# Stores of the split rows moved to GpSimd's queue, the second block's rows fetched two units later, two splits made first

## The chip, the cores and the metric

The kernel runs on one core of a Trainium2 chip. The metric is the device time of one execution in microseconds; the median of three runs is given, and one further execution was profiled. The engines are named as in the profile: PE (TensorE's matmuls; PEld its weight loads), DVE (VectorE), ACT (ScalarE), POOL (GpSimd) and SP (SyncE, which here only issues DMAs; SPq is its queue). The 16 DMA engines of the core carry the transfers that a queue issues.

## The reference, cut to what matters

```python
attn_out = _attn_ref(q, k, v)            # 4 batches, 8 heads, 576 tokens, 64 channels a head; masked softmax attention
x = attn_out.transpose(0, 2, 1, 3).reshape(2304, 512)
h = np.maximum(np.maximum(x @ w1, x @ w2), x @ w3)   # 512 -> 768, three gates, their maximum
x = h @ w_out                                        # 768 -> 512
h = x @ w_in                                         # 512 -> 2048
g = np.maximum(h, 0.0) + alpha * np.minimum(h, 0.0)
out = g @ w_out2                                     # 2048 -> 512
```

All tensors are float32.

## The kernel before, in words

Every float32 matmul is made of three: an operand is split into a high part (a cast to the matmul's type `F32R`, on ACT) and a low part (operand minus high part, on DVE or GpSimd), and `PAIRS` (L728) multiplies high by high, high by low and low by high. `split` (L231) is that pair of instructions; in the profile its cast is L233 and its subtraction L236.

The program has three stretches. In the first, a planner (`Weave`) orders attention for all four batches and the first net (the three gates and `w_out`) for batches 0 to 2. The results of the first net are stored to DRAM (`x2d`, by `store_x2`). The second stretch is `last_net(3)` (L844), the first net for batch 3, written as a generator whose units are run one by one by the loop at L1126. The third is the second net, over three blocks of 768 tokens (L1469 on); its products are made by a scheme with seven half-size products in place of eight (`PRODUCTS`), which needs sums of quarter matrices.

`last_net` has 12 gate units (n = 0 to 11, L740), then six rounds k = 3 to 8 of seven products each (n = 12 to 53, L922), then eight output units (n = 54 to 61, L762). The rounds use the seven-product scheme too, so batch 3's tokens are summed first: `row_sums` (L863) writes quarter sums on DVE in units 1 to 4, and `make` splits them. There are eight such factors: T1, T2, T3 and T4, each for two column halves i. T1 lies in the tile of the row sums itself (a tile of the pools `xsp` for i = 0 and `xst` for i = 1), T2 to T4 in temporaries. The first product of a round is copied from its PSUM bank by ACT (L940); DVE adds the others to it (L902), and in rounds 5 and 8 the result goes through a cast (L935) and a subtraction (L909) to become `h`, which the output units read. There are eight PSUM banks, so PE can be eight products ahead of the engines that empty them.

Beside these units the loop prepares block 1 of the second net (tokens 768 to 1535), in two halves (0 and 1). `early_load` fetches a half's four row tiles from `x2d` (L991, SP's queue), `early_sums` makes its four sums on GpSimd (L1000, tiles `t` and `xs`), and `early_split` splits its seven factors, one every second unit, with the cast on ACT (L233, `xst<-xs` and `xst<-t`) and the subtraction on GpSimd (L236). `early_store`, called one unit after each split, stores the finished tile to DRAM (`xd`, L1029, SP's queue). The split tiles come from two pools of two buffers, taken in turn, so the fifth split of a half waits for the first's store to land. `X_SPLIT` sets the units: the load of half 0 stands at unit X_SPLIT - 8, its sums at X_SPLIT - 2 and its seven splits from unit X_SPLIT on; half 1 follows 21 or 22 units later. The two loaded tiles of a half lie in the two buffers of `xsp`, where the row sums for i = 0 lie before and the rows of block 0 come after (`load_x2` at L1139).

Block 2 is prepared in the same way in the second net (`high_part` on ACT, `low_part` on DVE), and `early_store` serves it as well, 14 stores for each block. Each engine runs its instructions in the order of the program, and so does SP's queue: an issue that waits holds up all issues behind it.

Of the kernel before, what the change touches and what calls it, by code (L numbers as in the profile page):

```python
# [10 lines left out]
F32 = mybir.dt.float32  # L11
F32R = mybir.dt.float32r
# [10 lines left out]
P = 128  # L23
# [5 lines left out]
HALF = S // 2  # L29
# [20 lines left out]
NOW = 9  # L50
NG = 3 * NF1 // 2
NP = 3
X_SPLIT = 10
COST = (250, 600, 500, 500)


# [116 lines left out]
def attention_maxout_prelu_kernel(  # L173
# [13 lines left out]
    nc = tc.nc  # L187
# [43 lines left out]
    def split(hi, lo, src, hi_engine, lo_engine):  # L231
        if hi_engine is nc.scalar:
            hi_engine.copy(hi, src)  # L233
        else:
            hi_engine.tensor_copy(hi, src)
        lo_engine.tensor_tensor(out=lo, in0=src, in1=hi.bitcast(F32), op=ALU.subtract)  # L236
# [5 lines left out]
    def pool(stack, name, bufs, side="left"):  # L242
        return stack.enter_context(tc.tile_pool(name=name, bufs=bufs, side=side, reuse_waits="tile"))
# [5 lines left out]
    xd = [None] + [[[dram.tile([P, 2, HB], F32, name=f"xd{blk}_{k}_{i}") for i in range(2)]  # L249
                    for k in range(7)] for blk in range(1, NBLK)]  # L250
# [7 lines left out]
    xp = pool(x0x, "xp", 10)  # L258
# [486 lines left out]
    def gate_unit(b, hf, f, g, st):  # L745
        acc = gate_products(b, hf, f, g)
        if g == 0:
            st["t"] = tp.tile([P, HALF], F32, tag="t", name="t")
            nc.scalar.copy(st["t"], acc)
        else:  # L750
            nc.vector.tensor_tensor(out=st["t"], in0=acc, in1=st["t"], op=ALU.max)
        if g == 2:
            h = hp.tile([P, 2, HALF], F32R, tag="x", name="h")
            split(h[:, 0], h[:, 1], st["t"], nc.scalar, nc.vector)
            st["h", hf, f] = h
# [29 lines left out]
    def units(gates):  # L785
        hf = 0
        for what in gates:
            if what is None:
                yield from ((hf, None, dc) for dc in range(NCC))
                hf += 1  # L790
            else:
                yield from ((*what, g) for g in range(3))
# [51 lines left out]
    def last_net(b):  # L844
# [3 lines left out]
        def load_factors(k):  # L848
            if k < NG:
                for i in range(2):  # L850
                    t = words["s", k, i] = hw.tile([P, 2, DM], F32R, tag="w", name="w")
                    nc.sync.dma_start(t.bitcast(F32), sd[k - NP][i][:, :, :])
            else:
                n, i = divmod(k - NG, 2)
                load_h(n, ((0, 2), (1, 3))[i])
# [4 lines left out]
        named, row_sums = [], []  # L860
# [4 lines left out]
        for i in range(2):  # L865
            for r in range(2):
                for h in range(2):
                    x = xt[b, i + 2 * r, h].bitcast(F32)
                    later(rows[i][r][:, h, :HALF], x[:, 0], x[:, 1], ALU.add)
        temps = [[temp() for _ in range(3)] for _ in range(2)]  # L870
        for i in range(2):
# [4 lines left out]
            named += [("T1", i, b12), ("T2", i, t2), ("T3", i, t3), ("T4", i, t4)]  # L876
            for c, (name, h) in enumerate((("11", 0), ("21", 0), ("22", 1))):
                factors[name, i] = xt[b, i + 2 * (c > 0), h]
        named.sort(key=lambda it: ("T2", "T3", "T1", "T4").index(it[0]))

        def make(m):
            name, i, x = named[m]
            t = factors[name, i] = (xt[b, i, 1] if name == "T4" else
                                    (xp if m < 2 else tf).tile([P, 2, HALF], F32R, tag="x", name="x"))
            split(t[:, 0], t[:, 1], x, nc.scalar, nc.vector)

        for n, (hf, f, g) in enumerate(units(GATES_LAST)):
            gate_unit(b, hf, f, g, st)
            if n > 0:
                for step in row_sums[:4]:  # L890
                    step()
                del row_sums[:4]
            if 5 <= n < 11:
                make(n - 5)
            if n in (3, 5, 7):
                load_factors(NP + n // 2)
            yield
        for m in range(6, 8):
            make(m)
# [11 lines left out]
        for k in range(NP, NG):  # L911
# [5 lines left out]
            def product(w, off, name):  # L917
                bank_ = bank()[:, :HALF]
                m = 0
                for c in range(2):  # L920
                    for wi, xi in PAIRS:
                        nc.tensor.matmul(bank_, w[:, wi, off + c * P:off + (c + 1) * P],  # L922
                                         factors[name, c][:, xi, :], start=m == 0, stop=m == 5)
                        m += 1
                return bank_
# [12 lines left out]
            x = product(w0, 0, "11")  # L938
# [3 lines left out]
            x = product(sb, 256, "T2")  # L942
# [4 lines left out]
            x = product(w0, 256, "21")  # L947
# [3 lines left out]
            x = product(sb, 0, "T3")  # L951
# [4 lines left out]
            x = product(w1_, 256, "T4")  # L956
# [4 lines left out]
            x = product(sa, 0, "T1")  # L961
# [5 lines left out]
            x = product(sa, 256, "22")  # L967
# [50 lines left out]
    def early_load(blk, i, pool, tag):  # L1018
        early_rows[blk, i] = load_x2(blk, i, pool, tag)

    def early_sums(blk, i):
        sum_x2(blk, i, early_rows.pop((blk, i)), nc.gpsimd)
# [3 lines left out]

    def early_store():
        for blk, k, i, t in early_parts:
            nc.sync.dma_start(xd[blk][k][i], t.bitcast(F32))  # L1029
        early_parts.clear()  # L1030

    def fetch_x2(blk, k):
# [81 lines left out]
    tf = pool(sx, "tf", 4, "right")  # L1114
# [7 lines left out]

    ready = {X_SPLIT + 22 * half + 2 * k: (1, half, k) for half in range(2) for k in range(7)}
    gates = 3 * len(GATES_LAST) + 7 * (NG - NP)
    fetched = [gates - 1 + i for i in range(9)]
    for n, _ in enumerate(last_net(B - 1)):  # L1126
        if n in fetched:
            load_ow()
        if n - 1 in ready:
            early_store()  # L1130
        for half in range(2):
            if n == X_SPLIT + 21 * half - 8:
                early_load(1, half, xsp, "xs")
            if n == X_SPLIT + 22 * half - 2:
                early_sums(1, half)
        if n in ready:
            early_split(*ready[n], (xst, xsu)[n // 2 % 2])
        if n == gates - 5:
            rows = [load_x2(0, 0, xsp, "xs"), load_x2(0, 1, xst, "xst")]  # L1139
        if n == gates - 1:  # L1140
            sx.close()
            x0x.close()
            xmp = pool(ctx, "xmp", 1, "right")
        if n == gates:
            sum_x2(0, 0, rows[0], nc.vector)
        if n == gates + 1:
            sum_x2(0, 1, rows[1], nc.vector)
        for i, ks in {0: [(0, range(7))], 2: [(1, range(4))], 3: [(1, range(4, 7))]}.get(n - gates, []):
            for k in ks:
                x2h[0, k, i] = split_x2(0, k, i, xmp, f"x{k}{i}")  # L1150
# [291 lines left out]
    def low_part(half, k):  # L1442
        t, x = high_parts.pop((half, k))
        nc.vector.tensor_tensor(out=t[:, 1], in0=x, in1=t[:, 0].bitcast(F32), op=ALU.subtract)
        early_parts.append((2, k, half, t))
        if (half, k) != (0, 6):
            early_store()
# [12 lines left out]
    for half in range(2):  # L1460
        for n, i in steps[half][:4]:
            at(n, i, lambda: sums_left.pop(0)())
        for k, (n, i) in enumerate(steps[half][4:]):
            at(n - (i == 1), 4 if i == 1 else 2, lambda half=half, k=k: high_part(half, k))
            at(n, i, lambda half=half, k=k: low_part(half, k))
    at(NQ - 1, 0, early_store)

    outs = iter(())
    for n in range(NQ * NBLK):  # L1469
        blk, q = divmod(n, NQ)  # L1470
# [72 lines left out]
```

## Time and profile before

| what | us |
|---|---|
| median of three runs (lowest, highest) | 733.48 (731.77, 735.46) |
| the profiled execution's own time | 733.57 |
| its span, first to last instruction | 731.8 |
| PE busy in the span | 718.0 |
| DVE busy | 615.7 |
| ACT busy | 445.1 |
| POOL busy | 29.6 |

The span is 1.8 us shorter than the time of the same execution. Busy times are sums over the whole span. A row of a timeline gives the start, the length of a merged run of equal instructions, the engine and line, the tile written and the tiles read, and the idle time of the engine just before, with what ended it. For a DMA the row stands at its issue on SP's queue, and its length there is the issue alone.

### The profile page before, as it was taken

The page shows a single profiled execution, that of the slowest core. Times are in us where ns is not written, and L with a number is a line of the kernel's source. Part 1 is how long each engine was busy: PE and PEld are TensorE (multiplying, and loading weights), DVE is VectorE, ACT ScalarE, POOL GpSimd, SP SyncE. Part 2 cuts the span into 40 slices and gives each one's busy share as a digit, 9 for nine tenths or more (in the row PEclk, how much of TensorE's full clock was granted, in tenths as well). Part 3 has the DMA queues.
Part 4 walks back from the last instruction along what each step waited for, and adds up shares of the span by engine and source line. Part 5 has one row for each costly group of instructions (what it writes and reads, how often), then busy time and mean ns, then how long its engine had stood idle before and what let it go on. Part 6 is the DMA issues. An engine that isn't in the chain of part 4 may idle for free.

```text
span 731.8 us, 18170 instructions
## 1 busy us (share of the span) xinstructions
PE 718.0 (98%) x6682; PEld 698.6 (95%) x6682; DVE 615.7 (84%) x1680; ACT 445.1 (61%) x1180; POOL 29.6 (4%) x53
## 2 busy tenths in 40 slices
PE   8999999999999999979999999999999999999998
PEld 5899999999999999978999999999999999999997
DVE  6998987887989997749778988979888888888896
ACT  7988975876775784232355675626566644656561
POOL 2000000000000000056000000000000000000000
PEclk9999999999999999999999999999999999999999
DMA  8777499878999688688999799999788999877362
GB/s 294 274 267 233 176 315 336 321 275 305 326 345 352 240 278 290 203 315 318 364 316 337 259 329 324 403 379 378 242 308 317 369 400 359 297 232 257 113 192 80
DMA packets 90089, 214.46 MB, mean 293 GB/s; under 512 B 11152, under 2 KB 41360, under 8 KB 90000
## 3 DMA queue, kind: packets, MB, share of 16 engines
q1 hardware_dynamic: 90000, 213.30, 83.2%
q8 instruction: 53, 0.87, 0.5%
q14 instruction: 36, 0.29, 0.1%
HBM read 157.16 MB, written 56.10 MB: 291 GB/s over the span
## 4 chain that ended last, share of the span: by engine, by line
PE 90%; DMA 4%; ACT 3%; DVE 1%; issue 1%; SPq 0%; POOL 0%; ACTq 0%; DVEq 0%; POOLq 0%
PE bank L740 26%; PE ph L1378 23%; PE po L1179 15%; PE bank L762 8%; PE po L1185 4%; PE ph L1179 4%; PE bank L922 2%; PE po L1189 2%; DMA w<-ws 2%; PE bank L426 1%; PE bank L352 1%; PE bank L465 1%; DMA xs<-x 1%; DMA xd<-xst 1%; ACT es L487 1%; PE bank L535 1%
## 5 line engine op out<-in xcount | busy, mean ns | idle before, releaser
L1378 PE MATMUL ph<-x,w 128*128 128x384 f32 x990 | 199.4, 336 | 0.0
L740 PE MATMUL bank<-x,w 128*128 128x288 f32 x1440 | 197.7, 297 | 0.2 <-DVE w L286 0.2
L740 PEld LDWEIGHTS bank<-x,w 128*128 128x128 f32 x1440 | 191.9, 189 | 1.7 <-DVE w L286 0.4
L1378 PEld LDWEIGHTS ph<-x,w 128*128 128x128 f32 x990 | 166.6, 188 | 0.9
L1179 PE MATMUL po<-w,g 128*128 128x256 f32 x936 | 135.9, 282 | 0.0
L1179 PEld LDWEIGHTS po<-w,g 128*128 128x128 f32 x936 | 130.1, 190 | 0.3
L1384 DVE TENSOR_TENSOR c<-ph,c 128x384 f32<-128x384 f32 x165 | 89.3, 554 | 31.4 <-PE ph L1378 27.3
L1172 ACT CAST g<-c 128x384 fp32r<-128x384 f32 x93 | 47.0, 505 | 91.3 <-DVE c L1362 52.3
L762 PE MATMUL bank<-h,w 128*128 128x288 f32 x576 | 80.1, 297 | 0.0
L762 PEld LDWEIGHTS bank<-h,w 128*128 128x128 f32 x576 | 77.0, 189 | 0.5
L286 DVE TENSOR_TENSOR w<-word,w 128x512 fp32r<-128x512 f32 x100 | 63.5, 642 | 14.6 <-ACT w L283 13.7
L283 ACT CAST w<-word 128x512 fp32r<-128x512 f32 x100 | 57.5, 587 | 27.8 <-DMA wp<-w 9.3
L1322 ACT ACTIVATE c<-c 128x384 f32<-128x384 f32 x96 | 50.5, 526 | 32.6 <-DVE c L1384 31.4
L1323 ACT ACTIVATE c<-c,nalpha 128x384 f32<-128x384 f32 x96 | 59.3, 618 | 3.1
L1327 DVE SCALAR_TENSOR_TENSOR c<-c 128x384 f32<-128x384 f32 x96 | 53.0, 552 | 5.8 <-ACT c L1323 5.8
L1173 DVE TENSOR_TENSOR g<-c,g 128x384 fp32r<-128x384 f32 x96 | 52.8, 550 | 0.9 <-ACT g L1172 0.5
L1173 DVE TENSOR_TENSOR g<-k,g 128x384 fp32r<-128x384 f32 x72 | 37.0, 551 | 7.4 <-ACT g L1172 7.4
L922 PE MATMUL bank<-x,w 128*128 128x288 f32 x252 | 37.2, 308 | 5.7 <-ACT t L940 2.5
L1185 PE MATMUL po<-w,g 128*128 128x512 f32 x120 | 42.8, 396 | 0.0
L922 PEld LDWEIGHTS bank<-x,w 128*128 128x128 f32 x252 | 35.5, 197 | 7.3 <-ACT t L940 3.0
L590 ACT ACTIVATE word<-raw 128x512 f32<-128x512 f32 x56 | 36.9, 675 | 5.3 <-DMA raw<-in_w 5.0
L1362 DVE TENSOR_TENSOR k<-c 128x384 f32<-128x384 f32 x72 | 37.9, 550 | 0.0
(123 smaller groups left out, 897.7 us busy)
## 6 DMA issues: line engine op xcount, KB each, us to landing
w<-wh SPq DMA_DIRECT2D x72, 512.0 KB, 5.4
raw<-in_w SPq DMA_DIRECT2D x50, 512.0 KB, 5.2
w<-wo SPq DMA_DIRECT2D x48, 512.0 KB, 5.8
w<-wp SPq DMA_DIRECT2D x36, 512.0 KB, 6.3
wh<-w SPq DMA_DIRECT2D x24, 512.0 KB, 4.9
xd<-xst SPq DMA_DIRECT2D x28, 384.0 KB, 3.5
x<-xd SPq DMA_DIRECT2D x28, 384.0 KB, 8.2
ws<-w SPq DMA_DIRECT2D x12, 512.0 KB, 4.7
```

Of the source, the lines that this page charges most:

```text
L283: (nc.scalar.copy if e == "ACT" else nc.vector.tensor_copy)(out_, in_)
L286: nc.vector.tensor_tensor(out=out_, in0=x, in1=y, op=ALU.subtract)
L740: nc.tensor.matmul(acc, words["gate", f, g][:, wi, cc * P:(cc + 1) * P], xt[b, cc, hf][:, xi, :], start=n == 0, stop=n == 3 * NCC - 1)
L762: nc.tensor.matmul(acc, words["mix", f][:, wi, dc * P:(dc + 1) * P], st["h", hf, f][:, xi, :], start=n == 0, stop=n == 3 * NF1 - 1)
L922: nc.tensor.matmul(bank_, w[:, wi, off + c * P:off + (c + 1) * P], factors[name, c][:, xi, :], start=m == 0, stop=m == 5)
L1173: return g, lambda: nc.vector.tensor_tensor(out=g[:, 1], in0=x, in1=g[:, 0].bitcast(F32), op=ALU.subtract)
L1179: nc.tensor.matmul(bank[:, NH * half:NH * (half + 1)], g[:, gi, t * P:(t + 1) * P], w[:, wi, off:off + NH], start=first and i == 0, stop=l ...
L1185: nc.tensor.matmul(bank.rearrange("p (s n) -> p s n", n=NH), g[:, 0, t * P:(t + 1) * P], w[:, :, off:off + NH], start=first, stop=last)
L1323: nc.scalar.activation(a, a, AF.Copy, scale=nalpha[:, f:f + 1])
L1327: nc.vector.scalar_tensor_tensor(out=a, in0=h, scalar=0.0, in1=a, op0=ALU.max, op1=ALU.add)
L1378: nc.tensor.matmul(bank, words["h", n, i][:, wi, off + c * P:off + (c + 1) * P], x2h[blk, k, c][:, xi, :], start=m == 0, stop=m == 5)
L1384: nc.vector.tensor_tensor(out=out_, in0=bank, in1=other, op=ALU.add)
```

## The change

```diff
@@ -50,7 +50,7 @@
-X_SPLIT = 10
+X_SPLIT = 12
@@ -876,12 +876,12 @@
-        named.sort(key=lambda it: ("T2", "T3", "T1", "T4").index(it[0]))
+        named.sort(key=lambda it: ("T1", "T2", "T3", "T4").index(it[0]))
 
         def make(m):
             name, i, x = named[m]
             t = factors[name, i] = (xt[b, i, 1] if name == "T4" else
-                                    (xp if m < 2 else tf).tile([P, 2, HALF], F32R, tag="x", name="x"))
+                                    (tf if m < 4 else xp).tile([P, 2, HALF], F32R, tag="x", name="x"))
@@ -890,8 +890,8 @@
-            if 5 <= n < 11:
-                make(n - 5)
+            if 4 <= n < 10:
+                make(n - 4)
@@ -1026,7 +1026,7 @@
     def early_store():
         for blk, k, i, t in early_parts:
-            nc.sync.dma_start(xd[blk][k][i], t.bitcast(F32))
+            nc.gpsimd.dma_start(xd[blk][k][i], t.bitcast(F32))
```

The six splits T1 to T3 stand one unit earlier, T1 first; T1 and T2 take tiles of `tf`, T3 the two spare tiles of `xp`. Loads, sums and splits of block 1 stand two units later. All 28 stores of `early_store` are issued on GpSimd's queue.

On ACT, in rounds 3 to 5 of `last_net`, this stands before (`t<-bank` L940 is a round's first copy; `xst` are the seven split tiles of half 0 of block 1):

```order
L940 COPY t_5700<-bank_5693 128x288
L233 CAST xst_5702<-t_5626 128x384
L233 CAST xst_5723<-xs_5497 128x384
L233 CAST xst_5745<-t_5627 128x384
L233 CAST xst_5770<-xs_5496 128x384
L940 COPY t_5780<-bank_5773 128x288
L233 CAST xst_5792<-t_5628 128x384
L233 CAST xst_5814<-xs_5497 128x384
L940 COPY t_5864<-bank_5857 128x288
```

and this now:

```order
L940 COPY t_5696<-bank_5689 128x288
L233 CAST xst_5698<-xs_5540 128x384
L233 CAST xst_5719<-t_5661 128x384
L233 CAST xst_5741<-xs_5541 128x384
L233 CAST xst_5766<-t_5662 128x384
L940 COPY t_5776<-bank_5769 128x288
L233 CAST xst_5788<-xs_5540 128x384
L233 CAST xst_5810<-t_5663 128x384
L233 CAST xst_5834<-xs_5541 128x384
```

The first split has moved behind round 3's copy (it stood ahead of it), and the fifth (`xst_5770` before, `xst_5788` now) behind round 4's.

On SP's queue, from the weights of round 3 on, this stands before (`w<-ws` are the weight sums of rounds 3 to 8, `xs<-x2` the rows of block 1, `xd` the stores):

```order
L852 DMA w_5430<-ws3_1_150 128x1024
L991 DMA xs_5496<-x2_2_69 128x384
L991 DMA xs_5496<-x2_3_70 128x384
L991 DMA xs_5497<-x2_2_69 128x384
L991 DMA xs_5497<-x2_3_70 128x384
L852 DMA w_5521<-ws4_0_151 128x1024
L852 DMA w_5523<-ws4_1_152 128x1024
L852 DMA w_5563<-ws5_0_153 128x1024
L852 DMA w_5565<-ws5_1_154 128x1024
L852 DMA w_5602<-ws6_0_155 128x1024
L852 DMA w_5604<-ws6_1_156 128x1024
L1029 DMA xd1_0_0_121<-xst_5668 128x768
```

and this now:

```order
L852 DMA w_5430<-ws3_1_150 128x1024
L852 DMA w_5515<-ws4_0_151 128x1024
L852 DMA w_5517<-ws4_1_152 128x1024
L991 DMA xs_5540<-x2_2_69 128x384
L991 DMA xs_5540<-x2_3_70 128x384
L991 DMA xs_5541<-x2_2_69 128x384
L991 DMA xs_5541<-x2_3_70 128x384
L852 DMA w_5566<-ws5_0_153 128x1024
L852 DMA w_5568<-ws5_1_154 128x1024
L852 DMA w_5605<-ws6_0_155 128x1024
L852 DMA w_5607<-ws6_1_156 128x1024
L852 DMA w_5761<-ws7_0_157 128x1024
```

Round 4's weights stand ahead of the rows of half 0, and no store follows.

On POOL, from half 0's last sum on, every subtraction is now followed by its store (before, the seven subtractions stood in a row):

```order
L1000 TENSOR_TENSOR t_5663<-xs_5541,t_5661 128x384
L236 TENSOR_TENSOR xst_5698<-xs_5540,xst_5698 128x384
L1029 DMA xd1_0_0_121<-xst_5698 128x768
L236 TENSOR_TENSOR xst_5719<-t_5661,xst_5719 128x384
L1029 DMA xd1_1_0_123<-xst_5719 128x768
L236 TENSOR_TENSOR xst_5741<-xs_5541,xst_5741 128x384
L1029 DMA xd1_2_0_125<-xst_5741 128x768
```

The same holds for half 1. A subtraction thus stands behind the store of the one before it.

## Rows read from the trace of the kernel before

**Rows 1.** The page's first part: busy time, share and instructions of each engine.

```profile
PE 718.0 (98%) x6682; PEld 698.6 (95%) x6682; DVE 615.7 (84%) x1680; ACT 445.1 (61%) x1180; POOL 29.6 (4%) x53
```

**Rows 2.** Stretches: length; busy of PE, PEld, DVE, ACT, POOL; clock; DMA share; GB/s.

```profile
320.00:330.00 10.00, 8.41 (x60) 7.94 (x60) 2.52 (x4) 2.14 (x5) 6.27 (x7) 1.00 1.01 398
...
340.00:350.00 10.00, 9.08 (x57) 9.04 (x57) 9.38 (x19) 4.28 (x11) 8.97 (x9) 0.83 0.82 296
376.00:731.00 355.00, 352.39 (x2383) 346.39 (x2381) 305.82 (x654) 198.33 (x403) 1.72 (x3) 1.00 0.84 297
```

**Rows 3.** Timeline of PE in the rounds: start, length, line, tiles, idle before.

```profile
310.26 3.37 PE L922 MATMUL bank<-x,w 128*128 128x288 f32 x24
314.35 3.88 PE L922 MATMUL bank<-x,w 128*128 128x288 f32 x24 [0.72 <-ACT x L233]
319.90 5.86 PE L922 MATMUL bank<-x,w 128*128 128x288 f32 x42 [1.67 <-DMA w<-ws]
327.35 10.98 PE L922 MATMUL bank<-x,w 128*128 128x288 f32 x78 [1.59 <-ACT t L940]
338.98 1.06 PE L922 MATMUL bank<-x,w 128*128 128x288 f32 x6 [0.64 <-DVE t L902]
340.96 12.22 PE L922 MATMUL bank<-x,w 128*128 128x288 f32 x78 [0.92 <-ACT t L940]
353.01 19.38 PE L762 MATMUL bank<-h,w 128*128 128x288 f32 x144
```

**Rows 4.** Timeline of SP's queue (issues).

```profile
304.90 8.32 SPq L991 DMA_DIRECT2D xs<-x  x4
...
342.99 2.24 SPq L1029 DMA_DIRECT2D xd<-xst  x3
...
352.44 2.62 SPq L991 DMA_DIRECT2D xs<-x  x4
```

**Rows 5.** Timeline of ACT.

```profile
314.54 0.39 ACT L940 COPY t<-bank 128x288 f32<-128x288 f32 x1
...
326.49 0.51 ACT L233 CAST xst<-xs 128x384 fp32r<-128x384 f32 x1 [6.50 <-DMA xd<-xst]
326.90 0.39 ACT L940 COPY t<-bank 128x288 f32<-128x288 f32 x1
...
345.38 0.52 ACT L233 CAST xst<-xs 128x384 fp32r<-128x384 f32 x1 [2.94 <-DMA xd<-xst]
...
348.41 0.39 ACT L940 COPY t<-bank 128x288 f32<-128x288 f32 x1
```

**Rows 6.** Timeline of DVE.

```profile
306.63 0.46 DVE L863 TENSOR_TENSOR t<-xst,t 128x288 f32<-128x288 f32 x1
...
311.94 0.46 DVE L236 TENSOR_TENSOR x<-xs,x 128x288 fp32r<-128x288 f32 x1
...
327.33 1.02 DVE L902 TENSOR_TENSOR t<-bank,t 128x288 f32<-128x288 f32 x2 [8.79 <-ACT t L940]
...
350.69 1.01 DVE L902 TENSOR_TENSOR t<-bank,t 128x288 f32<-128x288 f32 x2
...
354.67 0.45 DVE L909 TENSOR_TENSOR h<-t,h 128x288 fp32r<-128x288 f32 x1
```

**Rows 7.** The split tiles: issues of their stores, ns min/median/max, first and last start.

```profile
L1029 SPq DMA_DIRECT2D xd<-xst x28: 319/320/572, 320.7 to 569.4; - x28
```

**Rows 8.** Timeline of POOL.

```profile
315.42 1.01 POOL L1000 TENSOR_TENSOR t<-xs 128x384 f32<-128x384 f32 x1 [308.47 <-DMA xs<-x]
...
319.65 1.00 POOL L236 TENSOR_TENSOR xst<-xs,xst 128x384 fp32r<-128x384 f32 x1
...
329.26 1.22 POOL L236 TENSOR_TENSOR xst<-xs,xst 128x384 fp32r<-128x384 f32 x1
337.23 1.01 POOL L1000 TENSOR_TENSOR t<-xs 128x384 f32<-128x384 f32 x1 [6.75 <-DMA xs<-x]
...
341.74 1.23 POOL L236 TENSOR_TENSOR xst<-xs,xst 128x384 fp32r<-128x384 f32 x1
```

## The prediction

> **What bounds the kernel now.** First the page's busy times: PE works 718.0 of 731.8 us [rows 1], so a change can give back only what PE stands idle or runs slowed, 13.8 us and a little clock. Second, where that is. In the second net, 376 to 731 us, PE is busy for 352.39 of 355 us [rows 2], and none of its instructions there has a wait beside it; block 2's 14 stores lie there, and moving them can only cost. What is left lies in the six rounds of last_net, from 310.26 to 353.01, 42.75 us for 42 products [rows 3]. The row at 327.35 has 78 matmuls (13 products) in 10.98 us, 0.845 us each, so 42 need 35.5 us. The other 7.25 are five waits (0.72, 1.67, 1.59, 0.64 and 0.92, together 5.54) and the clock: between 340 and 350 its mean is 0.83 of full speed [rows 2], 1.7 us lost, directly after the last two waits.
>
> Third, what each wait is, in the timelines. The 1.67 is for round 4's weights: on SP they stood behind the rows of half 0, which held the queue from 304.90 to 313.22 [rows 4] because a T1 split, DVE's `x<-xs` at 311.94, was still to read the tile that they overwrite [rows 6]. The 1.59 is for ACT's copy of round 4's first product, at 326.90; ACT had stood 6.50 us in the cast ahead of it, the fifth split, until the first split's store had landed [rows 5]. DVE stood 8.79 us for the same copy [rows 6], is busy 2.52 of 10 us there and 9.38 of 10 later [rows 2]; the 0.64 and the 0.92 are that backlog. The backlog also sets the end: the output units read `h`, and the second of the two low parts that the first unit needs last is ready at 354.67 + 0.45 = 355.12 [rows 6], 2.1 us after that unit began at 353.01. An output unit of 18 matmuls takes 19.38 / 8 = 2.42 us [rows 3] and asks for this part after 15 of them, 2.0 us in. So PE and DVE arrive together, and a gain must move both.
>
> **The change, part by part.** T1 first: the eight splits and their tiles' sizes stay, so DVE and ACT do as much work ahead of round 3; T2, the first needed, is made in units 6 and 7 and wanted in unit 13. Cost nothing, and the 0.72 for T4, which comes last as before, stays. The gain: T1's subtraction for i = 0 now stands directly behind the last row sum, which ends at 306.63 + 0.46 = 307.09 [rows 6], so it ends at 307.55 and not at 312.40. The last two loads of half 0 then leave by 307.55 + 0.82 = 308.4, not 313.22, and the sums on POOL, which began 2.2 us behind that (315.42) [rows 8], begin at about 310.6. Round 4's weights stand ahead of these loads on SP now: the 1.67 goes.
>
> Two units later: the first split stands behind round 3's copy (314.54 to 314.93) [rows 5] and the fifth behind round 4's. The copy that cost 1.59 us and DVE's 8.79 no longer waits for a store. What is late next is round 5's copy, behind the seventh split; PE has eight banks, 8 x 0.845 = 6.8 us, before it feels that. PE alone would thus run from 310.26 to 310.26 + 35.5 + 0.72 = 346.5, 6.5 us earlier than before. DVE, with no 8.79 us hole, follows.
>
> Stores on POOL: SP loses 28 issues and what waited behind them, which cost PE nothing but the 1.67. POOL gains seven stores in each half, each between two subtractions, and they hold up the subtraction behind them for a time d that no row shows. The least is an issue on SP, 0.32 us [rows 7]; the most is two subtractions, about 2.0 us (one, over 384 of the store's 768 columns, takes 1.00 to 1.23) [rows 8]. I take d = 1.0, one instruction of POOL itself, since descriptors made by an engine are nearer to its own work than to SP's issue. The chain of block 1, worked out with d:
> - Half 0. The first split ends at 314.93 + 0.51 = 315.4; POOL's sums (4.2 us, 315.42 to 319.65) [rows 8] are done before. Seven subtractions at 1.05 and six stores, each with 0.1 us of handover (an estimate: four sums of 1.01 us fill 4.23 us [rows 8], 0.05 lost at each), end at 315.4 + 7.35 + 6d + 0.6 = 323.4 + 6d. Before it was 329.26 + 1.22 = 330.5 [rows 8].
> - Half 1's last two loads wait for that: 0.8 us of issue and 2.4 us to land. Before, 6.75 us passed [rows 8], but with the DMA share at 1.01 [rows 2]; now the weights of rounds 4 to 6 are long through. Sums begin at 326.6 + 6d (337.23 before) and take 4.5 us, to 331.1 + 6d.
> - Three subtractions and three stores, 3.15 + 3d + 0.3, and the third store lands 2.5 us later (issue at 342.99, cast released at 345.38) [rows 4, 5]: the seventh split starts at 337.1 + 9d and round 8's copy 0.4 us later, at 337.5 + 9d (348.41 before) [rows 5].
> - From that copy, 0.4 us, and DVE's and ACT's steps to the second low part, 350.69 to 355.12 [rows 6]: ready at 342.3 + 9d. Before: 355.12.
>
> With d = 1.0 it is ready at 351.3, 3.8 us earlier than before. PE would be there at 346.5 + 2.0 = 348.5 and stands for about 2.8 us; I charge the clock loss seen after such a stand, 1.7 us. Net 3.8 - 1.7 = 2.1 us gained. The rows of block 0 wait for half 1's seventh subtraction: 331.1 + 7.35 + 0.6 + 12d = 339 + 12d, 351 at d = 1.0, still ahead of 352.44, where they left before [rows 4]. No loss. The second net follows without gaps.
>
> Sum: the profiled execution took 733.57 us, 1.8 beyond its span and 0.1 from the median of 733.48. 733.57 - 2.1 = **731.5 us**. In general the change is 9d - 11.1 us, floored at -6.5 by PE, and nothing at d = 1.23.
>
> On the first store's landing the row shows 5.8 us from its issue at 320.7 to the released cast [rows 5, 7], in a stretch with the DMA share at 1.01. The Trainium skill, in "DMA: Bandwidth & Descriptors", section "Issuing engines are not separate DMA queues", says that DMAs of all issuing engines run on the same 16 DMA engines and another issuer saves only issue time. That speaks against the move of the stores as such; the full share in that row agrees.
>
> **The rivals.** *The stores are cheap*, d below 0.83: nothing in the trace excludes 0.32. The chain then passes -3.6 us, and at d = 0.5 PE's floor decides: 733.57 - 6.5 = 727.1. Against it: POOL's shortest rows in the rounds are 1.00.
>
> *The stores choke POOL*, d above 1.64, where 9d - 11.1 passes +3.7: at d = 2.0 the change is +6.9, 740.5. The place is POOL between two subtractions of half 0 and half 1; nine of these intervals stand in the chain to round 8's copy. For it: DVE is busy 9.38 of 10 us while half 1 is split [rows 2], and POOL's subtraction took 1.23 where others took 1.00 [rows 8], so the two engines do disturb each other. The Trainium skill, in "SBUF — State Buffer", section "SBUF: two separate sides", tells of descriptors starved when VectorE runs in a mode with two ports. By it this rival would hold if DVE's subtractions here ran so; their rows, 0.46 us for 288 columns, don't tell.
>
> *The wait only moves*: the stores land no faster on their new queue, 5.8 us as the first did, not 2.5. With d = 1.0 the seventh split of half 1 is 3.3 us later, the gain of 2.1 becomes a loss of 1.2: 734.8. Against it: the row at 345.38 shows 2.4 us with SP [rows 4, 5].
>
> **How the numbers follow.** A difference of 0.5%, 3.7 us, is about what a measurement of this kernel can tell from none. The forecast (d from 0.83 to 1.64, quick landing) gets 0.35, cheap stores 0.33, choked stores 0.22, the moved wait 0.10. Faster is the second alone, 0.33; same is the first and last, 0.45; slower is 0.22. The range goes from PE's floor, 727.1, to d = 1.8 (733.57 + 5.1), 738.7; beyond lie the worse half of the choked stores and little else.
>
> **What would show it.** Right: PE without the waits at 319.90, 327.35, 338.98 and 340.96; POOL's sums of half 0 near 310.6; round 4's copy at PE's pace, near 318; one wait of PE inside the first output unit, for `h`; stores about 1.0 us apart from the subtractions around them. Read d from POOL: the spacing of half 0's subtractions less 1.15. Wrong: a first store that takes several us, round 5's copy that stops PE, a wait at the second net's first products for block 0's splits, or any wait of PE after 376, where the moved stores of block 2 could hold back ACT's casts.

## The result, and the profile after

The changed kernel takes **740.66 us** (median of four runs, 740.11 to 740.86) where the kernel before took 732.98 beside it: 1.0099 of it, 95% interval 1.0072 to 1.0127. That is slower by more than the 0.5% named ahead, and above the range. Measured again it took 739.33 against 734.32, 1.0069 (1.0045 to 1.0092), slower and above the range as well; that run's profile is called the second profile below. The profiled execution took 740.11 with a span of 738.0; 731.8 was the span before.

The page's first part answers to [rows 1]:

```profile
PE 720.7 (98%) x6682; PEld 700.4 (95%) x6682; DVE 619.8 (84%) x1680; ACT 445.7 (60%) x1180; POOL 45.0 (6%) x81
```

POOL has 28 instructions and 15.4 us more: the stores, 0.55 us each. The stretches answer to [rows 2] (columns as there):

```profile
320.00:330.00 10.00, 10.00 (x73) 10.00 (x73) 7.62 (x13) 2.06 (x5) 8.13 (x11) 0.96 0.82 287
...
340.00:350.00 10.00, 10.00 (x77) 10.00 (x76) 8.58 (x15) 2.66 (x6) 8.14 (x11) 1.00 0.73 262
350.00:360.00 10.00, 4.54 (x19) 3.43 (x18) 6.33 (x14) 2.35 (x6) 4.93 (x7) 0.75 0.81 280
356.00:361.00 5.00, 4.41 (x14) 3.54 (x15) 4.73 (x12) 2.04 (x6) 0.21 (x1) 0.50 0.99 313
...
376.00:731.00 355.00, 354.15 (x2383) 347.50 (x2382) 304.52 (x651) 199.20 (x405) 9.28 (x17) 1.00 0.84 295
```

From 320 to 350 PE now works without a gap, where before it was busy 8.41 and 9.08 of 10. Between 350 and 360 it works 4.54 of 10 at a mean clock of 0.75: there the gain is lost, and more. PE's timeline shows it, beside [rows 3]:

```profile
310.48 3.94 PE L922 MATMUL bank<-x,w 128*128 128x288 f32 x24
315.61 0.40 PE L922 MATMUL bank<-x,w 128*128 128x288 f32 x1 [1.19 <-ACT x L233]
316.96 0.69 PE L922 MATMUL bank<-x,w 128*128 128x288 f32 x3 [0.95 <-DVE x L236]
318.14 31.38 PE L922 MATMUL bank<-x,w 128*128 128x288 f32 x224 [0.49 <-DVE x L236]
349.35 1.78 PE L762 MATMUL bank<-h,w 128*128 128x288 f32 x12
356.09 1.34 PE L762 MATMUL bank<-h,w 128*128 128x288 f32 x3 [4.96 <-ACT h L935]
357.91 19.29 PE L762 MATMUL bank<-h,w 128*128 128x288 f32 x129 [0.48 <-ACT h L935]
377.04 2.27 PE L1378 MATMUL ph<-x,w 128*128 128x384 f32 x12
```

The four waits at 319.90, 327.35, 338.98 and 340.96 are gone. The 0.72 for T4 has become 2.63 in three pieces, and the first output unit, which had no wait, stands 5.44 us for `h`. PE reaches the output units 3.7 us earlier than before (349.35 against 353.01) and the second net 4.8 us later (377.04 against 372.23).

Why `h` is late is read backwards. Both waits of PE in the output unit end with ACT's casts for `h` (L935). ACT's round 8 copy (L940) stands behind the seventh split of half 1, beside [rows 5]:

```profile
347.52 0.51 ACT L233 CAST xst<-xs 128x384 fp32r<-128x384 f32 x1 [4.72 <-DMA xd<-xst]
349.11 0.51 ACT L233 CAST xst<-t 128x384 fp32r<-128x384 f32 x1 [1.08 <-DMA xd<-xst]
352.50 0.51 ACT L233 CAST xst<-xs 128x384 fp32r<-128x384 f32 x1 [2.87 <-DMA xd<-xst]
352.92 0.39 ACT L940 COPY t<-bank 128x288 f32<-128x288 f32 x1
355.61 0.43 ACT L935 CAST h<-t 128x288 fp32r<-128x288 f32 x1 [2.30 <-DVE t L902]
357.42 0.43 ACT L935 CAST h<-t 128x288 fp32r<-128x288 f32 x1 [1.39 <-DVE t L902]
```

The copy began at 348.41 before. The split waits for the third store of its half, whose buffer it takes over and which POOL issues at 347.65, beside [rows 8]:

```profile
314.42 0.99 POOL L1000 TENSOR_TENSOR t<-xs 128x384 f32<-128x384 f32 x1 [307.47 <-PE bank L922]
...
318.90 1.01 POOL L236 TENSOR_TENSOR xst<-xs,xst 128x384 fp32r<-128x384 f32 x1
320.24 0.70 POOL L1029 DMA_DIRECT2D xd<-xst  x1 [0.33 <-POOL xst L236]
320.96 1.02 POOL L236 TENSOR_TENSOR xst<-t,xst 128x384 fp32r<-128x384 f32 x1
...
330.48 1.02 POOL L236 TENSOR_TENSOR xst<-xs,xst 128x384 fp32r<-128x384 f32 x1
331.80 0.56 POOL L1029 DMA_DIRECT2D xd<-xst  x1 [0.30 <-POOL xst L236]
337.82 1.01 POOL L1000 TENSOR_TENSOR t<-xs 128x384 f32<-128x384 f32 x1 [5.47 <-DMA xs<-x]
...
342.18 1.01 POOL L236 TENSOR_TENSOR xst<-xs,xst 128x384 fp32r<-128x384 f32 x1
343.62 0.57 POOL L1029 DMA_DIRECT2D xd<-xst  x1 [0.42 <-POOL xst L236]
344.20 1.02 POOL L236 TENSOR_TENSOR xst<-t,xst 128x384 fp32r<-128x384 f32 x1
...
347.65 0.56 POOL L1029 DMA_DIRECT2D xd<-xst  x1 [0.41 <-POOL xst L236]
```

A store occupies POOL for 0.56 us (0.70 the first time) after a wait of 0.30 to 0.42 us for the end of the subtraction ahead of it. Subtractions are 1.90 us apart in half 0 and 2.02 in half 1. SP's queue answers to [rows 4]:

```profile
305.96 3.39 SPq L991 DMA_DIRECT2D xs<-x  x4
309.39 18.05 SPq L852 DMA_DIRECT2D w<-ws  x8
327.72 4.64 SPq L991 DMA_DIRECT2D xs<-x  x4
332.45 11.81 SPq L1043 DMA_DIRECT2D w<-wh  x6
```

The eight `w<-ws` are the weights of rounds 5 to 8; half 1's rows (327.72) now stand behind those of round 8, where before they stood ahead. And DVE:

```profile
315.65 2.43 DVE L236 TENSOR_TENSOR x<-t,x 128x288 fp32r<-128x288 f32 x2
...
354.39 1.18 DVE L902 TENSOR_TENSOR t<-t 128x288 f32<-128x288 f32 x1
...
358.04 0.45 DVE L909 TENSOR_TENSOR h<-t,h 128x288 fp32r<-128x288 f32 x1
```

The second low part of `h` is ready at 358.49 (355.12 before), 3.4 us later. The cast for that part ends at 357.85 and is what PE's last wait ends with; the low part is kept as the mark below because the prediction reckons by it.

### The profile page after: what moved, and what is told of

Same layout as the page of the kernel before. It is cut to its first block, busy times and chain, and to the rows that moved or that the text cites. A ratio compares the mean times of both kernels' runs of the same rounds, so it can differ in the third digit from the quotient of the medians.

```text
span 738.0 us, 18179 instructions
## 1 busy us (share of the span) xinstructions
PE 720.7 (98%) x6682; PEld 700.4 (95%) x6682; DVE 619.8 (84%) x1680; ACT 445.7 (60%) x1180; POOL 45.0 (6%) x81
## 3 DMA queue, kind: packets, MB, share of 16 engines
q0 software_dynamic: 2240, 11.01, 3.8%
## 5 line engine op out<-in xcount | busy, mean ns | idle before, releaser
L762 PE MATMUL bank<-h,w 128*128 128x288 f32 x576 | 83.1, 302 | 5.5 <-ACT h L935 5.4
L762 PEld LDWEIGHTS bank<-h,w 128*128 128x128 f32 x576 | 79.0, 193 | 7.0 <-ACT h L935 6.0
L830 DVE TENSOR_TENSOR t<-bank,t 128x288 f32<-128x288 f32 x72 | 32.6, 453 | 8.9 <-PE bank L740 5.1
```

What stands on the lines that cost most here:

```text
L762: nc.tensor.matmul(acc, words["mix", f][:, wi, dc * P:(dc + 1) * P], st["h", hf, f][:, xi, :], start=n == 0, stop=n == 3 * NF1 - 1)
```

## The experiments

Ratios are to the kernel before, measured beside each run; its medians there were 734.27 to 734.54 (732.98 beside the changed kernel's first measurement). In the recorded texts P says that the stores in POOL's stream are the loss, L the two later units, C the waits for T4 that T1 first brings.

### The three edits alone, and two together

Each edit by itself: `e1_t1` has the lines on T1 to T4 of the diff, `e2_later` has `X_SPLIT = 12`, `e3_pool` has

```diff
-            nc.sync.dma_start(xd[blk][k][i], t.bitcast(F32))
+            nc.gpsimd.dma_start(xd[blk][k][i], t.bitcast(F32))
```

and `e4_t1_later` the first two.

> The kernel before with one part of the change: the T1 splits made first, one unit earlier. Three theories. P: the loss comes from the stores in POOL's stream. L: it comes from the splits that stand two units later, so that round 8's copy waits longer behind half 1's last split. C: it comes from T1 first, because POOL's sums begin earlier and run into DVE's T4 subtractions, which PE then waits for (2.63 us about 315 us after, 0.72 before, and 1.7 us of clock). P and L expect no loss here: the wait of 1.67 us for round 4's weights goes, 731 to 733. C expects 735 to 737, with the waits about 315.

> The kernel before with X_SPLIT = 12 alone. P expects a gain: the fifth split stands behind round 4's copy, so the 1.59 us and DVE's hole of 8.79 us go, 728 to 732. L expects the loss, 737 to 741. C expects no loss, 730 to 733.

> The kernel before with the 28 stores on POOL's queue alone. P expects the loss, 737 to 742, with round 8's copy later than 348.4 and PE waiting for h at the first output unit. L and C expect 732 to 735.

> The changed kernel with the 28 stores back on SP's queue (T1 first and X_SPLIT = 12 stay). P expects a gain over the kernel before, 727 to 731. L expects 737 to 741. C expects 735 to 737.

| kernel | median | ratio (95%) |
|---|---|---|
| T1 first | 730.15 | 0.9945 (0.992 to 0.997) |
| two units later | 738.15 | 1.0056 (1.0034 to 1.0077) |
| stores on POOL | 741.72 | 1.0107 (1.0076 to 1.0138) |
| T1 first, two units later | 736.29 | 1.0025 (1.0009 to 1.004) |
| all three, first measurement | 740.66 | 1.0099 (1.0072 to 1.0127) |
| all three, again | 739.33 | 1.0069 (1.0045 to 1.0092) |

T1 first is a gain of 4 us, and the best of the parts. With it, two units later cost 0.8%, 5.9 us, and the stores another 0.44 to 0.74%, 3.2 to 5.4 us. So P and L both hold in part, and each fails where it expected no loss. C falls as the whole cause: T1 first alone has PE waits of 0.62, 1.18 and 1.10 us for T4 and is faster all the same. It also has no other wait of PE up to the output units:

```profile
318.55 32.89 PE L922 MATMUL bank<-x,w 128*128 128x288 f32 x227 [1.10 <-DVE x L236]
```

The profiled executions reach the rounds' first product at different times, so places in the rounds are compared from there (us; one execution each):

| kernel | first product | half 1's sums | round 8's copy | second net |
|---|---|---|---|---|
| before | 310.26 | +26.97 | +38.15 | +61.97 |
| T1 first | 310.85 | +24.40 | +35.81 | +59.88 |
| two units later | 311.30 | +29.14 | +42.77 | +66.10 |
| stores on POOL | 311.92 | +30.02 | +45.55 | +69.69 |
| T1 first, two units later | 311.86 | +26.14 | +39.87 | +63.22 |
| all three, first measurement | 310.48 | +27.34 | +42.44 | +66.56 |
| all three, again | 310.58 | +27.44 | +42.46 | +66.47 |

### One unit instead of two

`X_SPLIT = 11` with T1 first leaves half 1's rows ahead of round 8's weights on SP, and its third store ahead of the `wh` loads.

> The kernel before with T1 first and everything of block 1 one unit later (X_SPLIT = 11), stores on SP. Half 1's rows then still stand ahead of round 8's weights and its third store ahead of the wh loads, while half 0's rows stand behind round 4's weights, as in the changed kernel. Theory L in its narrow form (two units later cost because of these two places on SP's queue alone): half 1's sums near 335.3, no wait of PE in the output unit, time as with T1 first alone, 729.5 to 731. Rival (any delay of block 1 costs in proportion): half of the 6.1 us that two units cost with T1 first, 733.2.

731.47, just above what the narrow L gave, 0.9963 (0.9947 to 0.9979); with T1 first alone 0.9945, so one unit costs nothing that shows. Half 1's sums begin at 334.56 and round 8's copy at 345.62. With two units it was 338.00 and 351.73, of which 1.8 us is the later start of the rounds in that execution (311.86 against 310.06). The loss is not in proportion to the delay: it comes with the second unit, which moves two things past others on SP's queue. The rows move behind 1 MB of weights (sums 1.6 us later, counted from the rounds' first product) and the third store behind two `wh` loads (it leaves at 346.17 and lands 5.1 us later, not 342.1 and 3.0; from the sums to the copy 13.7 us instead of 11.1). The first move is tried by itself below, with the stores on POOL; the second was not.

### The rows of half 1, and what lies in the DMAs beside them

`e9_after_rows` is the changed kernel with these rows at unit 24, behind half 0's last split; `f2_after_hold` is the changed kernel with the `wh` loads held until unit 53; `f1_after` is the changed kernel again, beside `f2_after_hold`.

```diff
-            if n == X_SPLIT + 21 * half - 8:
+            if half == 0 and n == X_SPLIT - 8:
...
+        if n == X_SPLIT + 12:
+            early_load(1, 1, xsp, "xs")
```

```diff
-                n, i = divmod(k - NG, 2)
-                load_h(n, ((0, 2), (1, 3))[i])
...
+                held.append(k)
+                if k == NG + 3:
+                    for j in held:
+                        n, i = divmod(j - NG, 2)
+                        load_h(n, ((0, 2), (1, 3))[i])
```

> The changed kernel with one thing put back: the rows of half 1 are fetched at unit 24, behind half 0's last split and ahead of round 8's weights on SP (in the changed kernel they stand behind those weights). Theory L (the later fetch costs because the rows then land behind 1 MB of weights): half 1's sums begin at 335 instead of 337.82, round 8's copy at 350 instead of 352.92, PE's wait in the first output unit falls from 5.4 to about 2.6, time 737.5 to 738.5. Rival P (the rows wait for GpSimd's subtractions, at 331.5, and it is these and the stores between them that decide): the landing takes 5.5 us as before, the sums stay at 337.8, time 740.7.

> The changed kernel itself once more, beside the other runs of this call. If what the first runs showed is the whole of it: 1.0099 of the kernel before, with one wait of PE of 5 us or more in the first output unit and half 1's rows landing 6 us after half 0's last subtraction. If the profiled execution was a late one (its half 0's rows left at 305.96 us and landed at 314.42; with block 2's stores on SP the same code had 304.25 and 311.00): 738 to 739, and half 0's sums near 311 to 313.

> The changed kernel with the three pairs of wh loads that follow half 1's rows (2.8 MB, issued from 332 to 344) held until unit 53, where the fourth pair stands; nothing else moves. Theory D (the rows and stores of block 1 land late because the DMAs are full with weights that no engine needs yet): half 1's rows land 1 to 1.5 us sooner, the third store of half 1 in 3 instead of 4.3 us, round 8's copy 2 to 2.5 us sooner, time 2 to 3 us under the changed kernel's of this call. Rival W (they land late because of what is issued ahead of them, round 8's weights and half 0's stores): sums and copy within 0.7 us, time the same or, if the second net's first weights now come late, slower.

With the rows ahead of round 8's weights: 737.95, 1.0049 (1.0032 to 1.0066). Their four loads land in 4.9 us (median), against 6.1 in the profile after and 7.0 in the second one, and POOL's sums begin 6.0 us after half 0's last subtraction has ended, against 6.3 and 8.1. PE's waits in the output unit are 2.08, 0.79 and 0.23. The time is within what theory L gave, though its interval meets that of the changed kernel's second measurement. The rounds began late in the profiled execution (311.92), so the sums came at 336.85, not 335; counted from there they come at +24.93, 2.4 us earlier than in the changed kernel, round 8's copy 1.2 and the second net 1.7 to 1.8 us earlier (+41.26, +64.77). So the place of round 8's weights is a part of the loss, not the whole.

Holding the `wh` loads changes nothing for the better: 740.88, 1.0097 (1.0075 to 1.0119). The sums begin at 337.94, as rival W said, so the `wh` loads behind the rows don't hold them. What is left is what is issued ahead of them: round 8's weights, by the run above, and half 0's stores, which weren't tried apart. In the changed kernel the DMA share from 326 to 338 is 0.93, 1.00 and 1.02 in stretches of 4 us. The changed kernel measured again shows how little half 0 matters for these rows: its last subtraction ends 19.34 us after the rounds' first product, against 21.02 in the profile after, and the sums of half 1 begin at +27.44 and +27.34. Behind the sums the held kernel shows something else, in its stretch from 346 to 350:

```profile
346.00:350.00 4.00, 4.00 (x32) 4.00 (x31) 3.85 (x5) 1.03 (x2) 3.14 (x5) 1.00 0.51 198
```

The DMAs are half empty here, and the third store still takes 4.2 us from issue to landing. Finer stretches show that it isn't the transfer that is slow:

```profile
348.00:349.00 1.00, 1.00 (x10) 1.00 (x9) 0.97 (x2) 0.37 (x1) 0.98 (x2) 1.00 0.01 0
349.00:350.30 1.30, 1.30 (x12) 1.30 (x12) 0.89 (x1) 0.15 (x1) 0.89 (x2) 1.00 0.81 306
350.30:350.90 0.60, 0.60 (x6) 0.60 (x6) 0.00 (x0) 0.00 (x0) 0.58 (x2) 1.00 0.00 0
```

306 GB/s for 1.3 us is 398 KB, about one store, and then the DMAs stand still; the store issued at 347.96 has moved by 350.3, but counts as landed only at 352.2. The two stores ahead of it land within 0.5 us of the end of their transfers. The rows of this one store are, in the changed kernel, in the held one and in the kernel with T1 first and one unit (stores on SP):

```profile
L1029 POOL DMA_DIRECT2D xd<-xst x1: 557/557/557, 347.6 to 347.6; - x1
...
DMA to landing us min/median/max: 4.8/4.8/4.8
```

```profile
L1033 POOL DMA_DIRECT2D xd<-xst x1: 557/557/557, 348.0 to 348.0; - x1
...
DMA to landing us min/median/max: 4.2/4.2/4.2
```

```profile
L1029 SPq DMA_DIRECT2D xd<-xst x1: 320/320/320, 342.1 to 342.1; - x1
...
DMA to landing us min/median/max: 3.0/3.0/3.0
```

On SP the first three stores of half 1 land in 2.3, 2.4 and 3.0 us in this kernel as in the kernel before; on POOL, in the changed kernel, in 3.8, 3.4 and 4.8, and with the `wh` loads held in 2.6, 2.6 and 4.2. So for the first two most of the difference is the `wh` loads: on SP the second and third pair of these stood behind the first three stores (342.83 and 345.83 with one unit), and with the stores gone from that queue all six leave from 332.45 to 344.26.

### The stores on POOL, half by half

On the kernel with T1 first and one unit: all 28 stores on POOL (`f4_x11_pool`), only half 0's seven, only half 1's seven.

```diff
+            (nc.gpsimd if (blk, i) == (1, 0) else nc.sync).dma_start(xd[blk][k][i], t.bitcast(F32))
```

> T1 first and block 1 one unit later, as in the run before (731.5 against 734.3 of the kernel before, stores on SP), and now all 28 stores on GpSimd's queue: the stores alone change. Theory P (a store holds up the next subtraction by 0.75 to 0.87 us, and each half has seven in the chain to round 8's copy): half 0's subtractions end at about 329.5 instead of 326.9, half 1's sums begin 2.6 us later, at 337.2, the third low part is 1.7 us later again and its store lands in about 4 us instead of being done in time: round 8's copy at 350.5 to 351 instead of 345.6, time 735.5 to 737.5. Rival L (what costs is only the two units): 731 to 732.5.

> T1 first, block 1 one unit later, and only the seven stores of half 0 on GpSimd's queue. With all stores there the same kernel took 736.6 (ratio 1.0034 to the kernel before), with none 731.5 (0.9963). Theory H1 (half 1's rows wait for the DMAs, not for half 0's last subtraction, so that half 0's stores on GpSimd are hidden; the price is in half 1): half 1's sums within 1 us of 334.6, round 8's copy near 345.6 to 346.5, ratio 0.996 to 0.998. Rival S (the sum of the prediction: six stores of half 0 and three of half 1 in the chain, 0.8 us each): half 1's sums 4 to 5 us later, round 8's copy near 350, ratio about 1.001.

> T1 first, block 1 one unit later, and only the seven stores of half 1 on GpSimd's queue. Theory H1: half 1's sums at 334.6, the third low part 2 us later than with SP, its store lands 4 to 5.5 us after its issue in place of 3.0, round 8's copy at 349.5 to 351, ratio 1.002 to 1.004, the whole price of 5 us. Rival S: three stores of 0.8 us, round 8's copy at 348, ratio 0.999.

| stores on POOL | median | ratio (95%) | half 1's sums | round 8's copy | between |
|---|---|---|---|---|---|
| none | 731.47 | 0.9963 (0.9947 to 0.9979) | 334.56 | 345.62 | 11.1 |
| half 0 | 732.23 | 0.9973 (0.9958 to 0.9988) | 334.78 | 345.51 | 10.7 |
| half 1 | 734.64 | 1.0000 (0.9983 to 1.0017) | 336.98 | 353.13 | 16.2 |
| all 28 | 736.60 | 1.0034 (1.0018 to 1.0049) | 334.56 | 350.62 | 16.1 |

With all 28 the time is what P gave (735.5 to 737.5), but not by its way: it had the sums at 337.2. Half 0's stores are hidden, as H1 says: they end its subtractions about 2 us later, but the rows land at the same time. (With half 1's on POOL the rounds of the profiled execution began 2.2 us later, at 312.30, which is why its sums stand at 336.98.) Half 1's add 5 us between sums and copy: the third subtraction ends at 344.18 (with all on POOL) instead of 342.07, and its store, 5.5 us from issue to landing, holds the seventh split until 350.20. On SP that split waited for nothing but POOL. With half 1 alone the ratio lies between H1 and S. From the rounds' first product the second net comes 3.39 us later with half 1's stores on POOL and 3.25 with all than with none, in these profiles the same; the medians show 2.7 and 5.2 us. Where the difference of 2.5 lies isn't shown. Block 2's stores may hold it, but `e6_pool_b1`, the changed kernel with these 14 on SP again, is not clearly faster:

> The changed kernel with block 2's 14 stores back on SP; block 1's 14 stay on GpSimd. Theory P2 (in the second net the stores on GpSimd's queue land later, three of ACT's casts wait 4.0 us for them and PE stops for it): those waits go, the second net takes 359.0 to 359.7 us in place of 360.96, time 739.0 to 739.5. Rival (the second net's 1.4 us come from where it starts, not from its stores): it stays at 361 and the time at 740.7.

738.7, 1.0058 (1.004 to 1.0075), against 1.0069 and 1.0099. Its second net takes 359.6 us, where P2 put it. But that of the changed kernel takes 361.0 in one profile and 359.3 in the other. The casts of ACT that wait for stores there (six, 7.1 us together, in the first profile, with one wait of PE of 0.59; five, 5.1 us, in the second) do not stop PE every time.

### The waits for T4

`e10_after_t4` is the changed kernel with T4 as the last product of round 3; `e11_t1_t4` and `e13_t1_t4_x11` have the same in the kernels with T1 first, without and with one unit; `f6_t1_t4_x11_hold` also holds the `wh` loads.

```diff
+            if k == NP:
+                x = product(sa, 256, "22")
...
+                x = product(sa, 0, "T1")
...
+                x = product(w1_, 256, "T4")
```

> The changed kernel with the products of round 3 in another order: 22 and T1 stand ahead of T4, so T4's split has two products (1.7 us) more. Theory L or P (what decides is the seventh split of half 1 and with it h for the first output unit): PE's waits at 315 to 318, 2.6 us, shrink by 1.7 or more, and its wait in the output unit grows by as much; time 740.7, within 0.7. Rival C (the T4 waits and the clock they cost are the loss): 736.4 to 739.

> T1 first at the units of the kernel before, stores on SP, T4 as the last product of round 3. As in the run beside it: if the T4 waits are worth something, 2 us under T1 first alone (ratio 0.9945), 0.991 to 0.993; if h binds at once, 0.9945. Which of the two units is better shows whether half 0's rows should stand ahead of or behind round 4's weights.

> T1 first, block 1 one unit later, stores on SP, T4 as the last product of round 3; the wh loads where they were. Held wh loads made PE stand 3.9 us after 367 for a copy of ACT; without the hold that wait goes. If PE's waits for T4 (3.6 us in the run with T1 first and one unit) are worth something where h is ready in time: ratio 0.991 to 0.994, PE at the output units near 347 and a wait there of about 1 us. If h binds at once: 0.996, as without it.

> T1 first, block 1 one unit later, stores on SP, with T4 as the last product of round 3 and the wh loads held until unit 53. Where the T4 waits are the last thing that costs (PE waits 0.81, 0.51, 1.61 and 0.67 there and no more than 0.21 later): 1.7 us or more under 731.5, 728 to 730. Where h for the first output unit binds as soon as PE comes earlier: the waits move there and the time stays at 731 to 732.

In the changed kernel PE's waits for T4 fall from 2.63 to 0.90, it reaches the output units at 346.42 and stands there 5.6 us in place of 5.4. The time is 737.46, 1.0041 (1.0025 to 1.0056), below both measurements of the changed kernel and where rival C put it, though the interval meets that of the second. L and P expected the wait in the output unit to grow by what T4 gave back; it didn't, because `h` too came earlier (its second low part 45.70 us after the rounds' first product, against 48.01 and 47.98). So T4's waits may be up to 3 us of the changed kernel's loss. On the two faster kernels no gain shows: 729.15, 0.994 (0.9919 to 0.9961) against 0.9945, and 732.14, 0.9962 (0.9942 to 0.9983) against 0.9963. The last has the number expected if `h` binds, but another cause: PE comes 1.5 us earlier to the output units (3.4 counted from the rounds' first product), doesn't wait for `h`, and then waits 2.35 us for a copy of ACT (the line that is L978 in the changed kernel). These copies stand behind the splits of block 0 and then wait for the stores of earlier results to land (`x<-xo`, 1.02 and 1.22 us). Holding `wh` as well makes PE's wait 3.87 us (ACT's 1.83, 1.19 and 1.22) and the time 735.1, 1.0002 (0.9983 to 1.0021), above both expectations. That the `wh` loads, issued just ahead of these stores then, delay them is likely but not shown. The best kernels of all are those with T1 first alone, with or without T4 last.

## Why the prediction was wrong, point by point

The forecast was 731.5. The way to 740.1, in the profile after: the second low part of `h` at 358.49 instead of 351.3 (7.2 us), the clock's share of that loss 0.3 less than charged, the second net 1.4 longer than before, and 0.3 more around the span: 731.5 + 7.2 - 0.3 + 1.4 + 0.3 = 740.1. The 7.2 has four terms.

- **d was near, and a little too high.** 1.0 was taken; the spacings of 1.90 and 2.02 us less 1.15 give 0.75 and 0.87, on average 0.79. That is just inside the rival "the stores are cheap" (below 0.83), which was to be faster. With six and three of them the sum, 9d - 11.1, is a gain of 4.0 us, so it was the 11.1 that was wrong. "The stores choke POOL" had the sign and, with 740.5, even the time, but by a d of 2.0 that isn't there.
- **Half 0 starts late: +2.1.** The sums were to begin at 310.6. They began at 314.42 here, 311.95 in the second profile and 311.0 with block 2's stores on SP: with T1 first the rows land 2.7 to 5.1 us after their last issue, where 2.2 was taken. The DMAs are fuller now (share 0.92 to 1.02 from 304 to 314, where it was 0.04, 0.00 and 0.25 from 308 to 314 before); round 4's weights ahead of the rows are at most a part of it, since with T1 first alone, where they stand behind, it is 3.9. The first subtraction is at 318.90 instead of 315.4; the smaller d gives 1.4 back. In the second profile this term is 0.5.
- **Half 1's rows: +3.1, the largest and the decisive step.** The row of 6.75 us [rows 8] was replaced by 0.8 + 2.4, since "now the weights of rounds 4 to 6 are long through". But the change moves round 8's weights ahead of these rows on SP's queue, and half 0's own stores run then too. Measured were 6.3 us, 8.1 in the second profile, 6.0 with the rows ahead of the weights: the old row was the better price. In the second profile the terms are 0.5, 4.9, 1.1 and 0.7, so this one takes up what half 0 leaves, and the two together are 5.2 to 5.4: the sums of half 1 begin 27.3 and 27.4 us after the rounds' first product, as before (27.0), where the prediction's numbers give 22.3. The step that failed is thus the path: half 1's rows were taken to follow half 0's subtractions by 3.2 us, and they come when the DMAs have carried what is ahead of them. It also means that six of the nine d in the sum were hidden, as the run with half 0's stores alone shows.
- **The third store: +1.2.** 2.5 us from POOL's issue to the release of the cast was read from SP's row; it took 4.3 (352.50 less 348.21, where POOL's issue ends). The smaller d covers a part. This is "the wait only moves", which had 0.10, and for one store only.
- **From the copy to `h`: +0.8.** DVE's `t<-t` at 354.39 takes 1.18 us beside POOL's work, where 0.46 is usual.
- **T1 first** did more than was said: by itself it takes away all four waits, of which the prediction gave the last three to the two later units. "The 0.72 as before" was wrong: the T4 subtractions take 2.43 us for two (0.82 before), since POOL's sums now run at the same time, and round 4's copy came at 322.37, not near 318. What these waits cost in the changed kernel is 0 to 3 us, by the run with T4 last.
- **Two units later** was charged nothing beyond what it did on ACT. Its price is 0.8% with T1 first, and with the waits gone already it had nothing to gain there. The run with one unit puts the price down to the two moves on SP's queue; only one of them was tried by itself.
- **The clock** after the stand was charged with 1.7 us. From the low part of `h` to the second net it is 18.55 us against 17.11 before: 1.4. From 356 to 361 the granted clock is 0.50, its lower level, 1.2 GHz.
- **"The second net follows without gaps"** held in one profile and not in the other. Block 0's rows left at 351.29, as said (351).

The sentence cited from the Trainium skill, "DMA: Bandwidth & Descriptors", section "Issuing engines are not separate DMA queues", fits these runs: off SP's queue the stores land no sooner, but later (3.8, 3.4, 4.8 against 2.3, 2.4, 3.0 us). Its remark that only issue time is saved holds here for SP; POOL pays 0.56 us and a wait.

## What to carry to other kernels

When an edit changes the order on a DMA queue, price each transfer by the row that shows it under the same load, and don't lower it without counting the bytes that are then ahead of it. A store behind an instruction in order on a working engine costs the issue and the wait for the instruction ahead, here 0.8 us each, but only those count that lie between the last late arrival and the consumer. Try the parts of a change apart: here one of three was a gain of 4 us that the other two hid.

## What the runs showed of the hardware that was not expected

DVE's instructions with both inputs in SBUF slow down while POOL runs one of its own: `t<-t` over 288 columns takes 0.46 us alone, 1.18 at 354.39 and up to 1.67 elsewhere in the rounds of the profile after, and T4's two subtractions 2.43 instead of 0.82; those that read a PSUM bank stay at 0.45 to 0.5. The Trainium skill, "SBUF — State Buffer", section "SBUF: two separate sides", says that a DVE instruction with two SBUF inputs and a GpSimd instruction that reads SBUF exclude each other at a shared pair of ports; the rows agree. Its warning that descriptors starve while DVE runs in a mode with two ports doesn't show in these issues: those on POOL stay at 0.54 to 0.57 us but for the first (0.70).

That a store issued by POOL lands in 4.2 us with the DMAs half empty, where SP's needs 3.0 with the share at 1.01 to 1.02, was not expected either. 1.9 of the 4.2 us lie behind the end of its transfer; what they are, these runs leave open. The page counts POOL's stores on a queue of their own, q0, with 2240 packets, where SP's queue has 4032 fewer than before; whether that bears on it wasn't tested.
